# Attention into a soft mixture of experts: other order of the last second-layer weights, a plain output tail, and one weight pair loaded in pieces

## The chip, the core and the metric

The kernel runs on one core of a Trainium2 chip. The core has a matrix engine (PE, TensorE), a vector engine (DVE), a scalar engine (ACT), GpSimd (POOL), a sync engine (SP), and 16 DMA engines that move data between HBM and the on-chip SBUF. Matrix products land in PSUM, which has eight banks here. The metric is the device time of one execution in microseconds (us). Before the change three runs took 179.84, 180.31 and 181.1 us: a median of 180.31.

## The reference

Two stages are computed. The first is attention for 8 batches, 8 heads, 576 positions of 64 elements; four heads see the last 32 positions, four see every fourth of the last 128. The second is a soft mixture of experts over all 4608 tokens (x, 4608x512), with 8 experts of 4 slots each:

```python
logits = x @ phi                                  # 4608 x 32 slots
d = softmax(logits, over tokens); c = softmax(logits, over slots)
slot_input = d.T @ x                              # 32 x 512, 4 slots per expert
for e in range(8):
    h = np.maximum(slot_input[e] @ w1[e], 0.0)    # 512 -> 1024
    slot_out[e] = h @ w2[e]                       # 1024 -> 512
out = c @ slot_out                                # 4608 x 512, float32
```

Nothing of the output can be stored before every token is in `slot_input` and every expert's `w2` has arrived, since each output row mixes all 32 slots. The weights are 16 MB (w1) and 16 MB (w2) in float32 and are cast to bf16 by the transfers that load them; the output is 9.44 MB.

## The kernel before, in words

**Attention part.** Eight units (a pair of batches and a kind of mask each) go through transposes, scores, exponentials, masks, values and logits, with tiles in rotating buffers. The change doesn't touch this part. Its input is loaded unit by unit into three staging buffers (`stg`), all by transfers that POOL issues (`load_unit`, L415).

**Order of the work.** Every operation is entered with the function `op`: engine, what it reads and writes, a guessed cost and a key. A planner (`Prog.schedule`) then simulates the engines and writes out one fixed order for each; of operations that could start within 0.12 us it takes the smallest key. POOL's and SP's operations keep the order in which the program enters them. Where the planner sees PE idle between 116 and 149 us of its own time it puts in filler products (L1052), which compute nothing that is used. Waits are semaphore waits in front of an instruction, on the engine that executes it: whatever stands behind it on that engine waits too.

**Weights.** `wload` (L448) issues one transfer for a whole weight, or one for each listed piece (lo, hi, c0, c1): chunks lo to hi of the 1024 inner rows (8 chunks, each row of 128 partitions holds one per chunk) and columns c0 to c1. Weights go where buffers fall free. `w10` to `w16` have their own place (`WD`); `w17`, `w20` to `w24` use the three staging buffers, two in each; `w25` to `w27` use the attention's transposed tiles (`TT`). The last ones before the change are w25 whole, then for each half of the 512 output columns w26 with all 8 chunks, w27 with chunks 0–5, w27 with chunks 6–7. Behind them POOL issues 15 tiny copies, the "marks" (L782): mark n copies n rows of n elements, and nothing waits for them.

**Second stage.** When the attention is done, the slot inputs are folded (L794) and the first layer is multiplied (L814) into `h_sb`; L852 sums the token weights into `rtok`, and L832 and L841 turn `h_sb` into `hT`. The second layer (`ffn2`, L901) then makes, for each half of the output columns, one PSUM bank `sp_[h]` with the 32 slots: one product for each expert and chunk, 32 rows wide. Experts e and e+4 share one of four column groups of PE. All `ffn2` operations before the change stand in one chain, each after the one before it.

**Output tail before.** The function `half` handles one half of the columns. For chunks 6 and 7 of expert 7 it goes around the second layer: `h7` is scaled from `h_sb` (L871), multiplied with the first 512 tokens (L877) and evicted into `G` (L881, L884). `half` scales the unfinished slot outputs into `so_sb` (L931 or L932), multiplies the first two output groups by it (L957), adds the products of `G` with the late chunks (L960), and stores. Then the late chunks go through `ffn2` as well, rows 96–127 of the slot outputs are scaled once more into `so_fin`, POOL copies the other 96 rows there (L944), and the groups 1 to 5 follow (L989, evicted at L998 or L932). An output group of `half` is 256 tokens; its store (L926, on SP) is half the columns, 256 KB in 1 KB rows. There are six such groups (`NAB`). Last come groups of 512, 512, 1024 and 1024 tokens in full width (L1034), one store each.

Of the kernel before, what the change touches and what calls it, by code (L numbers as in the profile page):

```python
# [7 lines left out]
AluOp = mybir.AluOpType  # L8
# [294 lines left out]
def bass_dilated_sliding_attn__then__soft_moe_slots_kernel(  # L303
# [46 lines left out]
    so_fin = psA_sb[:].bitcast(BF16)[:, 0:DM]  # L350
    m7 = sb("m7", [128, 1], F32)
# [47 lines left out]
    b_m7 = Buf()  # L399
# [345 lines left out]

    W_AFTER = {2: ["w10"], 3: ["w11"], 4: ["w12"], 5: ["w13"], 6: ["w14"],
               7: ["w15", "w16"]}
    for u in range(NU):
        for j in range(4):
            st_T(u, j)  # L750
        if u + 3 < NU:
            for n_ in W_AFTER.get(u + 2, ()):
                wload(n_)
            load_unit(u + 3)
        else:
            if u == 5:
                for n_ in W_AFTER[7]:
                    wload(n_)
            for n_ in {5: ["w17", "w20"], 6: ["w21", "w22"], 7: ["w23", "w24"]}[u]:
                wload(n_)  # L760
        for i in range(6):
            st_S(u, i)
# [11 lines left out]
    for h_ in range(2):  # L774
        sl = (256 * h_, 256 * h_ + 256)
        wload("w26", ((0, 8) + sl,))
        wload("w27", ((0, 6) + sl, (6, 8) + sl))

    mk = sb("mk", [15, 136])
    for n_ in range(1, 16):  # L780
        o_ = sum(range(n_))
        op("pool", lambda g, n_=n_, o_=o_: [g.dma_start(mk[0:n_, o_:o_ + n_], moe_w2[7, 0:n_, 0:n_])],  # L782
           cost=0.3, sem=DmaSem(nc, f"s_mark{n_}"), nbytes=1024)
# [60 lines left out]
    NAB = 6  # L844
    GRP = [2] * NAB + [4, 4, 8, 8]
    rs = tile(psum, 1)

    def rsum(t):
# [13 lines left out]
    op("dve", lambda vv: vv.tensor_reduce(m7[:], ident[:, 100:104], mybir.AxisListType.X, AluOp.add),  # L862
       r=[b_id], w=[b_m7], cost=0.1, key=K1)
    op("dve", lambda vv: vv.tensor_tensor(m7[:], m7[:], rcs[:], AluOp.mult),
       r=[b_rcs], w=[b_m7], cost=0.1, key=K1)
    h7 = tile(pPT)
    G = [tile(pPT), tile(pPT)]

    def so_all(p0=0, p1=128, sl=slice(0, 512)):
        return so_fin[p0:p1, sl]  # L870
    op("dve", lambda vv: vv.tensor_scalar(sbt(h7)[:, 0:256].rearrange("p (f c) -> p f c", c=2),  # L871
                                          h_sb[:].rearrange("p (f c) -> p f c", c=8)[:, :, 6:8],
                                          m7[:, 0:1], None, op0=AluOp.mult),
       r=[b_m7] + b_h, w=[h7], alloc=[h7], cost=0.3, key=K1 + 1.5)
    for c in range(2):
        gp = tile(psum, 1)
        op("pe", lambda t, c=c, gp=gp: t.matmul(bank(gp)[:, 0:NG], sbt(h7)[:, c:256:2], expT[:, 0:NG],  # L877
                                                start=True, stop=True),
           r=[h7] + b_expT[:2], w=[gp], alloc=[gp, G[c]], cost=0.25, key=K1 + 1.6)
        if c == 0:  # L880
            op("act", lambda ac, gp=gp: ac.activation(sbt(G[0])[:, 0:NG], bank(gp)[:, 0:NG], ACTF.Copy),  # L881
               r=[gp], w=[G[0]], cost=0.6, key=K1 + 1.7)
        else:
            op("dve", lambda vv, gp=gp: vv.tensor_copy(sbt(G[1])[:, 0:NG], bank(gp)[:, 0:NG]),  # L884
               r=[gp], w=[G[1]], cost=0.6, key=K1 + 1.7)

# [4 lines left out]
    chain = []  # L891

    def ffn2(es_, lo, hi_, h_, key, after=()):
# [3 lines left out]
        def pe(t):  # L897
            for cc in range(lo, hi_):
# [8 lines left out]
               a=[sp_[h_], b_sp[h_]], cost=0.12 * (hi_ - lo), mode="c", key=key, after=chain[-1:] + list(after))  # L907
        chain.append(o)
# [11 lines left out]
    def store(d0, n, ap, ob, key, h_=None):  # L920
        so = DmaSem(nc, f"s_out{d0}_{h_}")
        s_out.append(so)
        dst = out[d0:d0 + 128 * n, :].rearrange("(p j) f -> p j f", j=n)
        if h_ is not None:
            dst, ap = dst[:, :, CH[h_]], ap[:, :, CH[h_]]
        op("sp", lambda e: [e.dma_start(dst, ap)], r=[ob], cost=0.1, sem=so,  # L926
           nbytes=262144 * n // (1 if h_ is None else 2), key=key)
# [6 lines left out]
    pb7 = {c0: pb for l2, h2, c0, c1, pb in HOME["w27"][1].parts if l2 == 6}  # L934
    AB = [(256 * o, osts[o // 2][:, 1024 * (o % 2):1024 * (o % 2) + 1024].rearrange(
        "p (j f) -> p j f", j=2), b_ost[o // 2]) for o in range(NAB)]
    b_soah = [[Buf(), Buf()] for _ in range(2)]

    def half(h_, key):
        sl = CH[h_]  # L940
        eA, eB = (("dve", "act"), ("act", "dve"))[h_]
        xe = op(eA, lambda en: scaled(en, so_sb[:, sl], bank(sp_[h_])[:, 0:256], rcs[:, 0:1]),
           r=[b_sp[h_], b_rcs, sp_[h_]], w=[b_so[h_]], cost=0.45, key=key)
        op("pool", lambda g: g.tensor_copy(so_all(0, 96, sl), so_sb[0:96, sl]), r=[b_so[h_]],  # L944
           w=[b_soah[h_][0]], after=b_psA.ready + b_psA.reads, cost=0.6, key=key + 0.1)
        po = [tile(psum, 1) for _ in range(3)]
        last = [None, None, None]
        for c in (None, 0, 1):
            for o in range(2):
                for j in range(2):  # L950
                    k_ = j if o == 0 else 2
                    d0 = AB[o][0]

                    def pe(t, o=o, j=j, k_=k_, d0=d0, c=c):
                        d_ = bank(po[k_])[:, CH[j] if o else CH[0]]
                        if c is None:
                            return t.matmul(d_, row(d0, 2)[j], so_sb[:, sl],  # L957
                                            start=o == 0 or j == 0, stop=False,
                                            skip_group_check=True)
                        return t.matmul(d_, sbt(G[c])[:, d0 + j:d0 + 256:2], w2v[7][:, 6 + c, sl],  # L960
                                        start=False, stop=c == 1, skip_group_check=True)
                    x = op("pe", pe, r=[b_so[h_]] + b_expT[:2] if c is None else [G[c], pb7[sl.start]],
                           a=[po[k_]], alloc=[po[k_]] if last[k_] is None else [], cost=0.15,
                           key=key + 1 + (0 if c is None else 1 + o) + 0.1 * j,
                           after=[last[k_]] if last[k_] is not None else [])
                    last[k_] = x
                    if c is not None:
                        HOME["w27"][1].reads.append(x)
        ffn2((7,), 6, 8, h_, key + 3.5, after=[xe])
        d0, ap, prev = AB[0]  # L970
        ob = Buf()
        for j in range(2):
            op(("act", "dve")[j], lambda en, j=j: scaled(
                en, AB[0][1][:, j, sl], bank(po[j])[:, 0:256], rtok[:, j:j + 1]),
               r=[po[j], b_rtok], a=[ob], after=prev, cost=0.4, key=key + 4)
        store(d0, 2, ap, ob, key + 4, h_)
        op(eB, lambda en: scaled(en, so_all(96, 128, sl), bank(sp_[h_])[96:128, 0:256],
                                 rcs[96:128, 0:1]),
           r=[b_sp[h_], b_rcs, sp_[h_]], w=[b_soah[h_][1]], after=b_psA.ready + b_psA.reads, cost=0.4, key=key + 4.1)
        for o in range(1, NAB):  # L980
            d0, ap, prev = AB[o]
            if o == 1:
# [122 lines left out]
```

## Time and profile before

| | |
|---|---|
| runs | 179.84, 180.31, 181.1 us (median 180.31) |
| profiled execution | 180.75 us, its span 179.0 us |
| PE busy | 136.4 us (76%) |
| DVE busy | 116.0 us (65%) |
| ACT busy | 94.1 us (53%) |
| POOL busy | 47.4 us (26%) |
| read from HBM, written | 61.94 MB, 9.44 MB |
| second layer L901 | 145.0 to 156.5 us |
| first store issued, last store issued | 151.55, 167.48 us |
| half-width stores, issue to landing | 3.4 us (median of 12) |

All times of the trace count from the start of the span. "Busy" is the time in which an engine executes; of a DMA transfer the profile gives the time of its issue on the engine that issues it, and the time to its landing. The trace also keeps when each transfer added to its semaphore: 16 additions, one from each DMA engine, so that one can see how far the engines stand apart. In the answers by stretches each row gives the length of the stretch, the busy time of PE, PEld (weight loads of PE), DVE, ACT and POOL, the granted clock of PE, the mean share of the 16 DMA engines, and GB/s.

### The profile page before, as it was taken

How to read it: one execution, taken by the hardware profiler on the slowest of the kernel's cores; microseconds unless marked ns; L12 is line 12 of the kernel's file. 1: busy time of each engine (PE TensorE's matmuls, PEld its weight loads, DVE VectorE, ACT ScalarE, POOL GpSimd, SP SyncE). 2: the span in 40 equal slices, each digit the busy share in tenths (PEclk: the TensorE clock that was granted, in tenths of full speed). 3: DMA queues.
4: the chain of work that ended last, by engine and by line, in shares of the span. 5: the costliest groups of instructions: out<-in, count | busy, mean ns of one | idle time of the engine just before them, and what ended most of it. 6: DMA issues, size and time to landing. Idle time of an engine off the chain costs nothing.

```text
span 179.0 us, 5831 instructions
## 1 busy us (share of the span) xinstructions
PE 136.4 (76%) x2614; PEld 104.3 (58%) x2614; DVE 116.0 (65%) x264; ACT 94.1 (53%) x141; POOL 47.4 (26%) x92
## 2 busy tenths in 40 slices
PE   0019789986988988898998698889999999879000
PEld 0019568865867967676876576865656587533000
DVE  6840297699579589759669669789952233489400
ACT  2004666975765894754895486675330121559300
POOL 7990700600700430620110010023995000000000
PEclk9999999999999999999999999999999999999855
DMA  5999999999999999999999999999999999889996
GB/s 81 192 216 212 216 214 212 222 214 212 219 210 210 217 214 217 208 226 207 220 208 220 211 216 222 212 211 223 212 211 213 194 198 118 251 293 396 421 458 293
DMA packets 13384, 40.81 MB, mean 228 GB/s; under 512 B 2352, under 2 KB 9520, under 8 KB 9520
## 3 DMA queue, kind: packets, MB, share of 16 engines
q0 software_dynamic: 8992, 30.94, 86.9%
q1 hardware_dynamic: 4368, 9.50, 14.1%
q8 instruction: 20, 0.33, 0.7%
q14 instruction: 4, 0.03, 0.0%
HBM read 61.94 MB, written 9.44 MB: 399 GB/s over the span
## 4 chain that ended last, share of the span: by engine, by line
PE 47%; DVE 28%; ACT 9%; DMA 5%; issue 3%; POOL 1%; DVEq 0%; POOLq 0%
DVE XB L651 9%; PE ps L549 7%; DVE PT L601 7%; DMA stg<-in_v_dram 5%; PE ps L544 5%; PE ps L695 5%; PE ps L611 5%; ACT PT L593 4%; PE ps L668 4%; DVE VN L616 4%; PE ps L586 3%; DVE WD L931 3%; PE ps L1052 3%; PE ps L901 3%; ACT TT L568 3%
## 5 line engine op out<-in xcount | busy, mean ns | idle before, releaser
L568 ACT ACTIVATE TT<-ps 128x864 f32<-128x864 f32 x32 | 28.6, 894 | 31.6 <-PE ps L549 22.5
L593 ACT ACTIVATE PT<-ps 128x768 bf16<-128x768 f32 x48 | 37.0, 813 | 8.4 <-PE ps L586 8.1
L549 PE MATMUL ps<-ident,stg 96*64 96x96 bf16 x576 | 18.3, 226 | 16.4 <-DMA stg<-in_v_dram 12.9
L651 DVE TENSOR_TENSOR XB<-ps,RV 96x768 bf16<-96x768 f32 x32 | 30.3, 948 | 0.7
L549 PEld LDWEIGHTS ps<-ident,stg 96*64 96x64 bf16 x576 | 16.0, 124 | 18.0 <-DMA stg<-in_v_dram 12.9
L616 DVE COPY VN<-ps 128x768 bf16<-128x768 bf16 x32 | 17.6, 548 | 11.8 <-PE ps L611 11.8
L415 POOL DMA_DIRECT2D stg<-in_q_dram x16 | 8.4, 533 | 46.1 <-PE ps L549 23.8
L640 PE MATMUL ps<-VN,PT 128*128 128x65 bf16 x384 | 18.1, 195 | 2.3 <-DVE PT L601 0.9
L611 PE MATMUL ps<-ident,TT 128*128 128x128 bf16 x192 | 17.7, 232 | 1.6 <-issue 0.9
L640 PEld LDWEIGHTS ps<-VN,PT 128*128 128x128 bf16 x384 | 14.8, 99 | 4.8 <-DVE PT L601 1.7
L586 PE MATMUL ps<-TT 64*128 64x96 bf16 x384 | 15.8, 211 | 2.0 <-ACT TT L568 1.0
L680 DVE COPY XT<-ps 128x576 bf16<-128x576 bf16 x17 | 10.1, 596 | 10.4 <-PE ps L668 10.3
L611 PEld LDWEIGHTS ps<-ident,TT 128*128 128x128 bf16 x192 | 11.8, 103 | 5.9 <-issue 2.3
L544 PE MATMUL ps<-ident,stg 96*128 96x96 bf16 x288 | 14.9, 206 | 0.2
L668 PE MATMUL ps<-ident,XB 96*128 96x96 bf16 x192 | 12.7, 207 | 2.5 <-DVE XB L651 2.2
L932 ACT ACTIVATE WD<-ps,rtok 128x256 f32<-128x256 f32 (+1 forms) x18 | 8.7, 591 | 9.5 <-PE ps L960 6.7
L586 PEld LDWEIGHTS ps<-TT 64*128 64x128 bf16 x384 | 10.1, 97 | 6.1 <-issue 1.7
L601 DVE TENSOR_TENSOR PT<-PT,mask_d 128x768 bf16<-128x768 bf16 x24 | 13.0, 544 | 0.9 <-ACT PT L593 0.4
L544 PEld LDWEIGHTS ps<-ident,stg 96*128 96x128 bf16 x288 | 13.0, 98 | 0.5 <-ACT PT L593 0.3
L448 POOL DMA_DIRECT2D stg<-in_moe_w_dram x6 | 3.2, 533 | 38.1 <-PE ps L544 25.5
L601 DVE TENSOR_TENSOR PT<-PT,mask_p 128x768 bf16<-128x768 bf16 x24 | 12.7, 541 | 0.4 <-ACT PT L593 0.4
L668 PEld LDWEIGHTS ps<-ident,XB 96*128 96x128 bf16 x192 | 9.5, 98 | 5.1 <-DVE XB L651 4.2
(95 smaller groups left out, 202.3 us busy)
## 6 DMA issues: line engine op xcount, KB each, us to landing
WD<-in_moe_w_dram POOLq DMA_DIRECT2D x7, 1024.0 KB, 26.2
stg<-in_moe_w_dram POOLq DMA_DIRECT2D x6, 1024.0 KB, 21.3
stg<-in_q_dram POOLq DMA_DIRECT2D x16, 288.0 KB, 16.2
stg<-in_k_dram POOLq DMA_DIRECT2D x16, 288.0 KB, 18.1
stg<-in_v_dram POOLq DMA_DIRECT2D x16, 288.0 KB, 20.1
out_dram<-WD SPq DMA_DIRECT2D x12, 256.0 KB, 3.4
out_dram<-WD SPq DMA_DIRECT2D x2, 1024.0 KB, 5.5
out_dram<-WD SPq DMA_DIRECT2D x1, 2048.0 KB, 8.8
```

What stands on the lines that cost most here:

```text
L544: i_ = t.transpose(bankb2(pt, a)[:, 96 * kk:96 * kk + 96], two[:, j // 2, c, :], ident[0:96, 0:96])
L549: i_ = t.transpose(bankb2(pt, a)[64 * hx:64 * hx + 64, 96 * kk:96 * kk + 96], src[:, hx, c, :], ident[0:96, 0:96])
L568: return ac.activation(d, sv, ACTF.Copy)
L586: i_ = t.matmul(pair(sc)[:, hx, QB * x:QB * x + QB], win(u, 1, h01, blk_, bpar)[64 * hx:64 * hx + 64], win(u, 0, h01, blk_, bpar)[64 * hx: ...
L593: op("act", lambda ac: ac.activation(sbt(pt)[:, 0:768].rearrange("p (x n) -> p x n", x=2), pair(sc)[:, :, 0:384], ACTF.Exp, scale=SCALE), ...
L601: return dv.tensor_tensor(p_, p_, m.unsqueeze(1).to_broadcast([128, 2, 384]), AluOp.mult)
L611: i_ = t.transpose(bankb(pv)[:, 128 * m:128 * m + 128], win(u, 2, h01, m, bpar), ident[:, :])
L616: op("dve", lambda dv: dv.tensor_copy(sbt(vn)[:, :, :, 0:64], bankb(pv)[:, 0:768].rearrange("p (m x d) -> p m x d", m=6, x=2)), r=[pv], w= ...
L640: i_ = t.matmul(pair(po)[:, bk, 65 * po_:65 * po_ + 65], sbt(pts[i])[:, o_:o_ + 128], sbt(vn)[:, m, half, 0:65], start=True, stop=True)
L651: op("dve", lambda dv: dv.tensor_tensor(sbt(xb)[:].rearrange("p m (x h d) -> p h x m d", x=2, h=2)[:, h01], pv()[:, :, :, 0:64], sbt(rv)[: ...
L668: i_ = t.transpose(bankb(px)[:, QB * m:QB * m + QB], sbt(xb)[:, m, 128 * x:128 * x + 128], ident[0:QB, 0:QB])
L680: return en.tensor_copy(d, s_)
```

## The change

Four things change.

1. The way around the second layer is taken out: `h7`, `G`, `m7`, `so_fin` and all that makes them. `half` now scales the finished slot outputs once into `so_sb`, and multiplies each group by it. The store of the first group is split in two of 128 KB.
2. `half` has five groups instead of six. A group of 256 tokens in full width (512 KB, 4 KB rows) stands ahead of the full-width groups.
3. The `ffn2` operations stand in a chain for each half, in smaller steps, and the last ones of the second half (expert 6's chunks 6–7, expert 7) are made dependent on the products of the first half's groups (`after=mm0`). w26 and w27 are loaded in other pieces.
4. The pair w23, w24 is loaded by `wpair` in six transfers in place of two: chunks 0–5 of both whole, then chunks 7 and 6 by rows, in pieces of 26, 102, 34 and twice 94 rows. Between them stand three tiny copies of 2, 2 and 7 rows (`turn`).

```diff
+    def turn(n):
+        i = len(turns)
+        turns.append(n)
+        op("pool", lambda g: [g.dma_start(
+            mk[0:n, i, :, 0:2],
+            moe_w2[7, 0:n, :].rearrange("p (a x) -> p a x", a=4)[:, 0:2, 0:2])],
+           w=[Buf()], cost=0.3, sem=DmaSem(nc, f"s_turn{i}"), nbytes=256)
+
+    def wpair(na, nb, s_, steps):
...
+        v_ = moe_w2[e0:e0 + 2].rearrange("e (p c) f -> p e c f", c=8)
+        d_ = stg[:, s_, 0:8192].rearrange("p (e c f) -> p e c f", e=2, c=8)
+        for n, st in enumerate(steps):
+            if isinstance(st, int):
+                turn(st)
+                continue
+            r0, r1, c0, c1, x = st
...
+            o = op("pool", lambda g, src=src, dst=dst: [g.dma_start(dst, src)],
+                   after=pb.prev, a=[pb], cost=0.6, sem=DmaSem(nc, f"s_{na}_{n}"),
...
-            for n_ in {5: ["w17", "w20"], 6: ["w21", "w22"], 7: ["w23", "w24"]}[u]:
+            for n_ in {5: ["w17", "w20"], 6: ["w21", "w22"], 7: []}[u]:
                 wload(n_)
+            if u == 7:
+                wpair("w23", "w24", 1, (
+                    (0, 128, 0, 6, None), (102, 128, 7, 8, None), 2, (0, 102, 7, 8, None), 2,
+                    (0, 34, 6, 7, None), 7, (34, 128, 6, 7, 0), (34, 128, 6, 7, 1)))
...
     wload("w25")
-    for h_ in range(2):
-        sl = (256 * h_, 256 * h_ + 256)
-        wload("w26", ((0, 8) + sl,))
-        wload("w27", ((0, 6) + sl, (6, 8) + sl))
+    wload("w26", ((0, 6, 0, 512), (6, 8, 0, 256)))
+    wload("w27", ((0, 4, 0, 256), (4, 8, 0, 256)))
+    wload("w26", ((6, 8, 256, 512),))
+    wload("w27", ((0, 4, 256, 512), (4, 8, 256, 512)))
...
-    NAB = 6
-    GRP = [2] * NAB + [4, 4, 8, 8]
+    NAB = 5
+    GRP = [2] * NAB + [2, 4, 4, 8, 8]
...
     def half(h_, key):
         sl = CH[h_]
+        mm = []
+        e0, e1 = (("dve", "act"), ("act", "dve"))[h_]
+        op(e0, lambda en: scaled(en, so_sb[:, sl], bank(sp_[h_])[:, 0:256], rcs[:, 0:1]),
            r=[b_sp[h_], b_rcs, sp_[h_]], w=[b_so[h_]], cost=0.45, key=key)
...
+        for o in range(NAB):
...
+            if o == 0:
                 for j in range(2):
...
+                    mm.append(op("pe", lambda t, j=j, p1=p1: t.matmul(
+                        bank(p1)[:, 0:256], row(0, 2)[j], so_sb[:, sl], start=True, stop=True),
+                        r=[b_so[h_]] + b_expT, w=[p1], alloc=[p1], cost=0.15, key=k2))
...
+                    store(d0, 2, ap, ob, k2, h_, j)
+                continue
...
+            mm.append(op("pe", pe, r=[b_so[h_]] + b_expT, w=[p2], alloc=[p2], cost=0.25, key=k2))
...
+            store(d0, 2, ap, ob, k2, h_)
+        return mm
+
+    for h_ in range(2):
+        k_ = K1 + 2 + 0.5 * h_
+        ffn2((0, 1, 2, 3), 0, 8, h_, k_)
+        ffn2((4, 5), 0, 4, h_, k_ + 2)
+        ffn2((4, 5), 4, 8, h_, k_ + 2.1)
+        ffn2((6,), 0, 6, h_, k_ + 4)
+    ffn2((6,), 6, 8, 0, K1 + 10)
+    ffn2((7,), 0, 4, 0, K1 + 11)
+    ffn2((7,), 4, 8, 0, K1 + 12)
+    mm0 = half(0, K1 + 20)
+    ffn2((6,), 6, 8, 1, K1 + 30, after=mm0)
+    ffn2((7,), 0, 4, 1, K1 + 31)
+    ffn2((7,), 4, 8, 1, K1 + 32)
     half(1, K1 + 40)
```

In the order that the planner writes for the changed kernel, all engines do the same as before up to the second layer. From there PE has five filler products ahead of the second layer instead of two products of `h7` and two fillers, and none ahead of the first output products, where three stood. Ahead of the first half's scaling now stand 118 second-layer products instead of 110. SP has 17 stores instead of 16.

## The prediction

> **What bounds the kernel now.** I read the slices of the whole span first, then the timeline of the tail, then the transfers' share by stretches. The slices:
>
> ```profile
> DMA  5999999999999999999999999999999999889996
> GB/s 81 192 216 212 216 214 212 222 214 212 219 210 210 217 214 217 208 226 207 220 208 220 211 216 222 212 211 223 212 211 213 194 198 118 251 293 396 421 458 293
> ```
>
> The 16 DMA engines are full from start to end but for the slices around 150 us (a slice is 4.5 us). Up to there they load (input bytes are counted after the cast to bf16); behind it they store 9.44 MB. The end is therefore the start of the stores, plus their transfer time, plus every hole in the stream. The timeline of the tail shows start and hole:
>
> ```profile
> 148.41 0.96 PE L901 MATMUL ps<-TT,hT 128*32 128x256 bf16 x12
> ...
> 149.41 0.48 DVE L931 TENSOR_SCALAR so_sb<-ps,rcs 128x256 bf16<-128x256 f32 x1 [4.03 <-PE ps L901]
> ...
> 150.40 1.04 PE L960 MATMUL ps<-TT,PT 128*128 128x256 bf16 x8
> 150.82 0.47 ACT L932 ACTIVATE WD<-ps,rtok 128x256 f32<-128x256 f32 x1 [5.75 <-PE ps L960]
> ...
> 151.55 13.63 SPq L926 DMA_DIRECT2D out_dram<-WD  x15
> ...
> 156.51 0.69 DVE L998 TENSOR_TENSOR WD<-ps,rtok 128x512 f32<-128x512 f32 x1
> 157.23 0.49 DVE L931 TENSOR_SCALAR psA_sb<-ps,rcs 32x256 bf16<-32x256 f32 x1
> 157.78 1.05 PE L989 MATMUL ps<-psA_sb,expT 128*128 128x256 bf16 x8 [0.99 <-DVE psA_sb L931]
> 158.21 1.29 DVE L998 TENSOR_TENSOR WD<-ps,rtok 128x512 f32<-128x512 f32 x2 [0.49 <-PE ps L989]
> ```
>
> The reader is to see two detours. In half 0 the slot outputs (so_sb) are ready to be scaled at 149.41, but the first store is issued only at 151.55, since the side products L960 lie between. In half 1 the outputs are scaled twice: DVE makes rows 96–127 again at 157.23, PE multiplies at 157.78, DVE evicts at 158.21. The stretches show what this does to the transfers (the last two figures are DMA share and GB/s):
>
> ```profile
> 157.00:159.00 2.00, 1.22 (x10) 0.93 (x10) 1.48 (x4) 0.57 (x2) 0.00 (x0) 1.00 1.04 349
> 159.00:161.00 2.00, 1.94 (x10) 0.81 (x8) 2.00 (x4) 2.00 (x5) 0.00 (x0) 1.00 0.66 223
> 161.00:163.00 2.00, 2.00 (x9) 0.67 (x8) 2.00 (x4) 2.00 (x5) 0.00 (x0) 1.00 1.04 345
> 163.00:168.00 5.00, 2.48 (x9) 0.78 (x8) 4.41 (x7) 3.94 (x7) 0.00 (x0) 1.00 1.05 429
> ```
>
> Half-width stores run at some 345 GB/s, full-width ones at 429, and between 159 and 161 a third of the time is lost. The trace's landing records (each transfer adds to its semaphore once per DMA engine) agree. The stores' landings are 153.9, 154.7, 155.8, 156.5, 157.3, 158.1, 158.9, 159.6, then 161.2, 162.0, 162.7, 163.5: 0.76 us apart, with holes of 0.35 (third) and 0.85 (ninth). The 1 MB stores follow at 2.5 us each, the 2 MB ones at 4.9 each; the last lands at 178.54.
>
> **The loads.** The same records show sixteen engines that do not finish together. Whole weights take 4.86 us per engine. w25 lands on eight engines from 138.27 to 139.45, on the other eight from 140.56 to 142.34; the last piece of w27 from 148.93 to 150.12 and from 151.50 to 153.06.
>
> **The change, part by part.**
>
> *Pieces of w23 and w24.* Chunks 6 and 7 of the pair are 512 reads of 2 KB, 32 per engine before. Now 8x34=272 go to eight engines and the other 240 to all, 15 each: 49 against 15. A read costs 76 ns (4.86 us/64 in a whole load) to 83 (two of the 512-byte packets, of which 64 took 2.67 us); I take 80. So 17x80 ns=1.36 us more on eight engines, and less on eight. Which eight, no row of before tells. If they are the early ones, w25 lands at 139.6–140.8 and 139.2–141.0; I take this, but an even spread leaves the sum as it is, as the cover below shows. Eight more small transfers stand in the queue. The nearest rows are the closing marks: their packets follow each other on an engine by 0.03 us, their landings by 0.18. That makes 0.2 to 1.4 us; I take 0.2, since the first store's data landed only 0.16 us behind the last mark on the late engines, so data does not wait in that line. w25 is in at 141.2 instead of 142.3. On POOL nine issues replace two: about 9x0.55=5 us from 117.44, done by 122.5, before w25's at 123.83 (which waits for PE); the engines hold earlier loads until 123.7. It costs nothing.
>
> *Order of w26 and w27.* Half 0 now needs 0.75 weight at whole-load speed (3.65 us) and 0.625 in 512-byte packets (5.34 us a weight, so 3.34) behind w25: 141.2+7.0=148.2 against 147.7 before. The last load lands 3.34 later, at 151.5 instead of 153.06.
>
> *Half 0 on PE.* Gone are G (two products of 0.22), h7, two evictions and POOL's copies; three more filler products of 0.22 stand in their place, so the second products start 0.2 later than 145.01. Ahead of the scaling now lie expert 6's chunks 0–5 of half 1 as well (6 matmuls) and 7's chunks 6–7 (2). Matmuls of one expert follow by 0.109 us; experts use separate column groups, and group 7 began some 0.4 us before 6 ended. Expert 6: 14 from 148.30, last at 149.72; expert 7: 8 from 149.4, last at 150.18; scaling 0.31 later, at 150.5 instead of 149.4. Bounds: 150.0 if 7 overlaps fully, 151.2 if not at all. The pieces that this waits for landed 1.6 us before their use; that is the cover. Without it each us of lateness is one of the end.
>
> *First stores.* 150.5+0.48 (scaling)+0.07+0.33 (product to eviction)+0.47=151.85; the first store issues at 151.9, 0.35 later than now, but with 128 KB. The next is another 128 KB; SP's price for that form is unknown, between 0.33 (128 rows) and 0.62 (256 rows), I take 0.45. The third (256 KB) issues at 152.85 and lands 2.25 later (1.5+0.755) at 155.1, and from there the transfers set the pace: SP issues every 0.62, ACT and DVE deliver two stores in about 0.8.
>
> *Half 1.* Ten half-0 products stand in front on PE's queue (the added dependency): 151.05 to 152.15; behind them wait ten FFN products, done by 153.3; ACT ends its evictions at 153.45 and scales until 154.05; product and eviction until 155.0; SP is free at 155.4. The stream would run dry only for an issue after 155.9. So the hole goes, and SP, then the transfers, are late next.
>
> *The sum.* Third store 155.1; three more, 157.4; half 1, 2x0.38+4x0.755, 161.15; the new 512 KB group 1.25 (a quarter of 4.9 to two half-width, 1.51), 162.4; 2x2.5, 167.4; 2x4.9, 177.2. That is 1.3 us before 178.54. The profiled execution took 180.75 (span 179.0 and 1.75 around it), so 179.45; it lies 0.44 above the median of 180.31, hence 179.0 there.
>
> **A rule against the rows.** The closing marks number the engines: mark n is n rows of 2n bytes, and the records hold n such packets, one per engine. By these, engines 0–4, 7 and 8 reached them at 148.6–149.9, 5, 6 and 9–14 at 151.3–152.9; 15, without data, is then the eighth early one. The Trainium skill ("DMA: Bandwidth & Descriptors", latency and other measured facts) says instead that engines 7 and 15 are usually the slow ones. By its section on why a DMA adds 16, a transfer takes the largest divisor of its rows up to 16 as its number of engines, from a rotating cursor: 26, 2, 102, 2, 34 rows from engine 0 put the 34-read shares on 15, 0–4, 7 and 8. By the rows these are the early eight, and the sum stands; by the rule on 7 and 15 two would be late, with half 0 in at about 150.9 and some 180.1 us. I go by the rows.
>
> **The rivals.**
>
> 1. *The change doesn't do what it says: no rebalancing, or the wrong eight.* Even spread: half 0 in at 142.34+0.2+7.0=149.5, still ahead of its use at 149.8. Late eight: 142.34+1.36+0.2+7.0=150.9, scaling at 151.65, 1.15 later: 180.1. 14%.
> 2. *More gain.* Experts 6 and 7 overlap fully, scaling at 150.0, and SP's short issues cost 0.33: 1.9 us, 178.4. If the half-width stores also go at 0.67 us apart, as the late engines did while they caught up (landings from 156.4 to 160.4), the eight 256 KB' worth of them behind the third store save 0.7 more: 177.7. For it: separate column groups. Against it: the 0.4 us of overlap seen, and the 0.76 of the other engines. 20%.
> 3. *Slower: reads piled on a late engine.* If the 94-row pieces go to two engines each, those take 47 reads more, 3.8 us. On a late engine half 0 lands at 142.34+3.8+0.2+7.0=153.3, scaling at 154.1, 3.6 later: +2.3, 182.6. It decides from a landing after 149.8, and makes the kernel slower from 151.1 on. 8%.
>
> **How the numbers follow.** Forecast 179.0, its own range 178.4 to 179.8, 58%. Range for 8 in 10: 177.7 to 181.0, from the second rival's best to the first's worst. One per cent (1.8 us) is about what a measurement here tells from no change: the three runs span 179.84 to 181.1. Faster by over 1% (under 178.5): rival 2 and the forecast's edge, 0.25. Slower by over 1% (over 182.1): rival 3, 0.07. The rest 0.68.
>
> **What would show it.** Landings of w25 within 2 us; scaling of half 0 at 150.5; first store at 151.9; no dip of the DMA share between 155 and 163; twelve landings without a hole; last landing at 177.2. Wrong it would be if half 0 waits for a landing, if 128 KB stores cost SP the full 0.62, or if the stores' pace changes.

## The result, and the profile after

The changed kernel took 178.68 us (median of seven runs, 178.51 to 179.21), the kernel before 179.87 us (seven runs, 179.46 to 181.1; the three known beforehand are among them). The ratio is 0.9912, with a 95% interval of 0.9883 to 0.994: 0.9% less time. Runs more than 1.5% above the fastest of their kernel are left out of the medians, ranges and ratios of this document. The profiled execution of the changed kernel took 178.78 us with a span of 177.0, against 180.75 and 179.0 before. In the profile after, the second layer is L912, the scaling L944 or L945, the products of `half` L962 and L975, its evictions L944, L945 and L987, the stores L939.

The slices of the whole span, transfers only (an average slice is 4.4 us now):

```profile
DMA  5999999999999999999999999999999999899996
GB/s 71 200 212 216 210 219 212 214 215 212 219 216 211 217 210 211 223 208 216 217 212 216 217 215 213 220 213 216 212 210 200 212 194 194 196 357 416 446 437 296
```

The valley of the profile before, 118 GB/s around 150 us and 251 and 293 behind it, is gone: the lowest value there is 194, and the next step is 357 at once. The stretches of the tail (length; busy time of PE, PEld, DVE, ACT and POOL; clock; share of the 16 DMA engines; GB/s):

```profile
151.00:153.00 2.00, 1.54 (x14) 0.71 (x11) 1.27 (x3) 1.59 (x5) 0.00 (x0) 1.00 0.69 120
...
157.00:159.00 2.00, 1.91 (x8) 0.64 (x8) 2.00 (x4) 2.00 (x5) 0.00 (x0) 1.00 1.06 356
159.00:161.00 2.00, 1.91 (x7) 0.65 (x8) 2.00 (x4) 2.00 (x5) 0.00 (x0) 1.00 1.06 392
```

The stretch from 159 to 161, where the transfers' share was 0.66 before, now has 1.06. One weak stretch is left, from 151 to 153. The timeline shows what stands at its front:

```profile
145.40 1.70 PE L912 MATMUL ps<-TT,hT 128*32 128x256 bf16 x14 [0.34 <-DMA TT<-in_moe_w_dram]
147.41 0.61 PE L912 MATMUL ps<-TT,hT 128*32 128x256 bf16 x4 [0.31 <-DMA TT<-in_moe_w_dram]
148.93 0.61 PE L912 MATMUL ps<-TT,hT 128*32 128x256 bf16 x4 [0.90 <-DMA TT<-in_moe_w_dram]
149.57 0.48 DVE L944 TENSOR_SCALAR so_sb<-ps,rcs 128x256 bf16<-128x256 f32 x1 [8.73 <-PE ps L912]
150.11 0.39 PE L962 MATMUL ps<-so_sb,expT 128*128 128x256 bf16 x2 [0.58 <-DVE so_sb L944]
...
150.94 9.74 SPq L939 DMA_DIRECT2D out_dram<-WD  x15
...
152.13 0.61 PE L912 MATMUL ps<-TT,hT 128*32 128x256 bf16 x4 [0.21 <-DMA TT<-in_moe_w_dram]
152.78 0.47 ACT L945 ACTIVATE so_sb<-ps,rcs 128x256 bf16<-128x256 f32 x1 [0.41 <-PE ps L912]
```

Before, each half had two scalings: half 0 at 149.41 and (rows 96–127) at 151.79, half 1 at 154.44 and 157.23. Now there is one in each half, the products follow it 0.54 us later, and the first store issues 1.37 us behind the scaling, where 2.14 us lay between. But three groups of the second layer now stand behind a weight that is still in flight (the brackets: 0.34, 0.31 and 0.90 us idle, ended by a DMA from `in_moe_w_dram`). The chain of waits, asked for the stretch from 120 to 160 us (start, duration, what), says the same:

```profile
120.00 4.72 POOL TT L445 x7
124.72 27.37 DMA TT<-in_moe_w_dram
152.09 0.04 issue
152.13 0.62 PE ps L912 x4
```

It runs along the loads alone, from their issue on POOL to the last landing at 152.09, and only then enters PE. In the profile before loads and PE changed places: DMA had 5% of the whole chain and PE 47%; here DMA has 21% and PE 27%.

### The profile page after: what moved, and what is told of

The parts are those of the page before. It is cut to its first block, busy times and chain, and to the rows that moved or that the text cites. A ratio compares the mean times of both kernels' runs of the same rounds, so it can differ in the third digit from the quotient of the medians.

```text
span 177.0 us, 5782 instructions
## 1 busy us (share of the span) xinstructions
PE 132.5 (75%) x2589; PEld 101.0 (57%) x2594; DVE 113.1 (64%) x258; ACT 93.0 (53%) x140; POOL 51.8 (29%) x98
## 4 chain that ended last, share of the span: by engine, by line
DVE 29%; PE 27%; DMA 21%; ACT 9%; POOL 4%; issue 2%; DVEq 0%; POOLq 0%
DMA TT<-in_moe_w_dram 15%; DVE XB L648 9%; DVE PT L598 8%; PE ps L546 5%; DMA stg<-in_v_dram 5%; PE ps L541 5%; ACT PT L590 4%; DVE VN L613 4%; PE ps L692 4%; ACT TT L565 4%; DVE WD L944 3%; PE ps L608 3%; POOL TT L445 3%; PE ps L665 3%; PE ps L583 3%
## 5 line engine op out<-in xcount | busy, mean ns | idle before, releaser
L637 PE MATMUL ps<-VN,PT 128*128 128x65 bf16 x384 | 17.6, 194 | 2.7 <-DVE PT L598 1.2
L608 PE MATMUL ps<-ident,TT 128*128 128x128 bf16 x192 | 16.3, 221 | 0.7 <-DVE VN L613 0.5
L583 PE MATMUL ps<-TT 64*128 64x96 bf16 x384 | 15.3, 204 | 1.2 <-ACT TT L565 1.0
L945 ACT ACTIVATE WD<-ps,rtok 128x256 f32<-128x256 f32 (+1 forms) x19 | 9.1, 605 | 10.3 <-PE ps L962 10.3
L608 PEld LDWEIGHTS ps<-ident,TT 128*128 128x128 bf16 x192 | 10.8, 98 | 4.7 <-issue 1.6
L583 PEld LDWEIGHTS ps<-TT 64*128 64x128 bf16 x384 | 9.6, 94 | 5.2 <-ACT TT L565 1.2
L678 ACT ACTIVATE XT<-ps 128x576 bf16<-128x576 bf16 x15 | 9.8, 650 | 3.8 <-PE ps L665 3.5
```

Of the source, the lines that this page charges most:

```text
L583: i_ = t.matmul(pair(sc)[:, hx, QB * x:QB * x + QB], win(u, 1, h01, blk_, bpar)[64 * hx:64 * hx + 64], win(u, 0, h01, blk_, bpar)[64 * hx: ...
L608: i_ = t.transpose(bankb(pv)[:, 128 * m:128 * m + 128], win(u, 2, h01, m, bpar), ident[:, :])
L637: i_ = t.matmul(pair(po)[:, bk, 65 * po_:65 * po_ + 65], sbt(pts[i])[:, o_:o_ + 128], sbt(vn)[:, m, half, 0:65], start=True, stop=True)
```

## The experiments

Two readings were set against each other. By the prediction's own, PE sets when half 0 is finished, the loads have 1.6 us of cover, and the pieces of w23 and w24 are worth nothing. By the other, which the profile after suggests, the last load of half 0 sets it, and the pieces are worth what they bring it forward. All ratios are against the kernel before on the same chip; its median was between 179.77 and 179.97 us in each group.

### The pieces taken out (e1_plainpair)

```diff
-                wpair("w23", "w24", 1, (
-                    (0, 128, 0, 6, None), (102, 128, 7, 8, None), 2, (0, 102, 7, 8, None), 2,
-                    (0, 34, 6, 7, None), 7, (34, 128, 6, 7, 0), (34, 128, 6, 7, 1)))
+                wload("w23")
+                wload("w24")
```

> The changed kernel with one part undone: w23 and w24 are loaded whole again (two transfers, no pieces, no turns). Theory A, the one of the prediction (the gain is the tail's: one scaling, no side products, no hole; the loads are covered): the time stays at the changed kernel's, 178.7 us, and half 0 is scaled at the same time as in it. Theory B (in the changed kernel PE waits 0.9 us for w27's last piece of half 0, so the loads set the start of the stores): the late eight engines end some 1.2 us later, half 0 is scaled at 150.8 instead of 149.57, and the time is 179.8 us.

Measured: 179.5 us (nine runs, 179.21 to 179.55), ratio 0.9967 (0.9953 to 0.998). The timeline of this kernel:

```profile
149.65 0.61 PE L911 MATMUL ps<-TT,hT 128*32 128x256 bf16 x4 [0.69 <-DMA TT<-in_moe_w_dram]
150.30 0.48 DVE L943 TENSOR_SCALAR so_sb<-ps,rcs 128x256 bf16<-128x256 f32 x1 [8.40 <-PE ps L911]
```

w25 again lands over 4.1 us (138.52 to 142.57) instead of 1.2 (140.25 to 141.43), the last load of half 0 at 149.61 instead of 148.88, and everything behind it moves by that 0.73: scaling 150.30, last landing 177.31 instead of 176.58. That is less than the 1.2 us of theory B, but its mechanism: the loads set half 0, and the pieces are worth 0.7 us here (0.8 by the medians), not nothing.

### The same pieces for the other eight engines (e2_wrong8)

```diff
-                    (0, 128, 0, 6, None), (102, 128, 7, 8, None), 2, (0, 102, 7, 8, None), 2,
-                    (0, 34, 6, 7, None), 7, (34, 128, 6, 7, 0), (34, 128, 6, 7, 1)))
+                    (0, 128, 0, 6, None), 6, (102, 128, 7, 8, None), 2, (0, 102, 7, 8, None), 2,
+                    (0, 34, 6, 7, None), 9, 8, (34, 128, 6, 7, 0), (34, 128, 6, 7, 1)))
```

Only the tiny copies between the pieces differ; their row counts set which engines the next piece goes to.

> The changed kernel with other turns (6 ahead of the 26 rows, 9 and 8 instead of 7 behind the 34 rows), so that the 34-read shares should fall on engines 5-10, 13 and 14: six of the eight that were late before, and two early ones. Theory A: 178.7 to 179.5 us. Theory B: w25's slowest landing goes from 141.4 to about 144, half 0 is scaled 2.5 us later, and the time is about 181.2 us. If the shares don't follow the turns, the landings of w25 look like those of the changed kernel.

Measured: 181.29 us (five runs, 181.15 to 181.42), ratio 1.0072 (1.0058 to 1.0087). The timeline:

```profile
151.45 0.61 PE L912 MATMUL ps<-TT,hT 128*32 128x256 bf16 x4 [0.78 <-DMA TT<-in_moe_w_dram]
152.10 0.48 DVE L944 TENSOR_SCALAR so_sb<-ps,rcs 128x256 bf16<-128x256 f32 x1 [7.63 <-PE ps L912]
```

w25 lands from 137.50 to 143.20, the last load of half 0 at 151.40, and the end moves by the same 2.5 us, as theory B had it. With the reads on six of the eight late engines and two early ones the kernel is slower than before: the prediction's first rival exists, at 181.3 instead of the 180.1 reckoned.

### The new tail over the old order of loads (e3_tailonly, e4_oldorder)

Both put the loads of w26 and w27 back to one half after the other; e3 also takes the pieces out as in e1. PE's order stays that of the changed kernel.

```diff
-    wload("w26", ((0, 6, 0, 512), (6, 8, 0, 256)))
-    wload("w27", ((0, 4, 0, 256), (4, 8, 0, 256)))
-    wload("w26", ((6, 8, 256, 512),))
-    wload("w27", ((0, 4, 256, 512), (4, 8, 256, 512)))
+    for h_ in range(2):
+        sl = (256 * h_, 256 * h_ + 256)
+        wload("w26", ((0, 8) + sl,))
+        wload("w27", ((0, 4) + sl, (4, 8) + sl))
```

> The new tail alone: w23 and w24 whole, w26 and w27 in the order of before (half 0 complete first, then half 1). Theory A: 178.7 us or less. Theory B: half 0 is complete at 147.7, so the first store is issued at about 149.9, but half 1's last load comes at 153.1 and its first store at 155.2, after the stream has run dry for 1.2 us: 178.9 us.

> The changed kernel with the pieces of w23 and w24, but w26 and w27 in the order of before (half 0 complete first). Theory A: no change, 178.7 us. Theory B: half 0 complete at 147.0 (141.4 and 5.3 for one weight in 512-byte packets), first store at about 149, last load at 152.1, half 1's first store at 154.3 instead of 154.5; a hole of about 1 us in the stream, but its end 0.7 us earlier: 178.0 us.

Measured: e3 181.14 us (five runs, 181.02 to 182.49; ratio 1.0091, 1.006 to 1.0122), e4 180.82 us (six runs, 180.22 to 181.22; ratio 1.005, 1.0033 to 1.0068). Both are far from what either reading gave. The timeline of e4 shows why for that kernel:

```profile
149.46 1.50 PE L912 MATMUL ps<-TT,hT 128*32 128x256 bf16 x16 [0.78 <-DMA TT<-in_moe_w_dram]
151.00 0.48 DVE L944 TENSOR_SCALAR so_sb<-ps,rcs 128x256 bf16<-128x256 f32 x1 [6.78 <-PE ps L912]
```

PE still has expert 6's chunks 0–5 of *half 1* ahead of half 0's last products. In the old order of loads that weight lands late (149.42), so half 0 waits for a load of half 1. These two edits did not undo one part; they broke a pair: the order of the loads and the order of the products must be changed together (the next two runs do that, and are 1.7 and 1.9 us faster). For e3 the profiled execution (184.0 us) had PE late for another reason, told at the end, so its wait is not shown there.

### The pair kept together (e5_tail2, e6_order2)

Both use the old order of loads with a fitting order of products; e5 without the pieces, e6 with them.

```diff
-        ffn2((6,), 0, 6, h_, k_ + 4)
-    ffn2((6,), 6, 8, 0, K1 + 10)
+    ffn2((6,), 0, 8, 0, K1 + 10)
...
-    ffn2((6,), 6, 8, 1, K1 + 30, after=mm0)
+    ffn2((6,), 0, 8, 1, K1 + 30, after=mm0)
```

> The new tail alone, now with PE's order made to fit the loads of before: w23 and w24 whole, w26 and w27 half by half, and all of expert 6's second half behind the first half's products (in the earlier run its chunks 0-5 stood ahead of them and waited for a load of half 1). Theory A (the gain is the tail's): half 1's last load at 153.1 sets its first store to 155.2, 0.7 us later than in the changed kernel, which delays the end by 0.25: 178.9 us. Theory C (the gain is the loads' alone: their order and their balance): 179.9 us, as before.

> The changed kernel (with the pieces) with w26 and w27 half by half and PE's order to fit. Theory B (loads set the start of the stores): half 0 complete at 147.0, scaled at 147.8 to 149.4 as PE arrives, last load 152.1, half 1's first store at 154.3 against 155.1 in the profile of the changed kernel; 178.0 us. Rival: the order of the loads only moves a wait from half 0 to half 1, 178.7 us.

Measured: e5 179.46 us (twelve runs, 179.29 to 181.01; ratio 0.9989, 0.9964 to 1.0013), between the ends written down, and not told apart from the kernel before; e6 178.9 us (seven runs, 178.68 to 179.2; ratio 0.9939, 0.9918 to 0.9961). So the new tail without the pieces is worth 0.3 us by the medians (179.46 against 179.77; the interval allows 0.65), and the pieces add 0.6. For e6 theory B's 178.0 did not come, its rival's 178.7 nearly did. In e6 the first store issues at 148.72, 2.2 us before that of the changed kernel, yet nothing is gained, and its last load lands later (152.37 against 152.09). The timeline of e6:

```profile
150.21 1.44 PE L912 MATMUL ps<-TT,hT 128*32 128x256 bf16 x12 [1.04 <-DMA TT<-in_moe_w_dram]
152.41 0.61 PE L912 MATMUL ps<-TT,hT 128*32 128x256 bf16 x4 [0.77 <-DMA TT<-in_moe_w_dram]
153.06 0.47 ACT L945 ACTIVATE so_sb<-ps,rcs 128x256 bf16<-128x256 f32 x1 [2.92 <-PE ps L912]
```

Half 1 waits for its loads, and is scaled 0.28 us later than in the changed kernel; its first store issues as early (154.43 against 154.46). The trace shows where the early start is lost. The first packets of the first store start 1.9 us after its issue (150.63), against 0.85 in the changed kernel (151.79) and 0.84 in e1: the store starts only as the loads leave the first of the DMA engines (last load landed there at 150.72). And the engines end apart: the last store is done on the first of the sixteen at 175.98, 0.40 earlier than in the changed kernel (176.38), but on the last one at 176.80, 0.82 later than on the first (0.20 in the changed kernel). So an engine that is still behind sets the end; I take it to be one that was late with the loads. The 15 marks stand on every engine between loads and stores; no run takes them out of e6, so their part in this is open.

### Six half-width groups as before (e7_nab6)

```diff
-    NAB = 5
-    GRP = [2] * NAB + [2, 4, 4, 8, 8]
+    NAB = 6
+    GRP = [2] * NAB + [4, 4, 8, 8]
```

On top of e6.

> As the one with order and pieces, and with six half-width groups instead of five, so that half 0 has 0.76 us more of stores to cover the wait for half 1's last load, at a price of 0.13 for each half (256 KB in 1 KB rows 0.76, in full width 0.63). Theory B: the hole of 0.9 us is filled, 177.6 us. Rival (no hole to fill): 0.26 us slower than the run with five.

Measured: 178.86 us (twelve runs, 178.74 to 180.56), ratio 0.9947 (0.9923 to 0.997): the same as e6. Theory B's 177.6 did not come, and the rival's 0.26 us is not seen either: the sixth group per half against the 512 KB group makes no difference that can be seen.

### The pieces in the old kernel (e8_before_pieces)

The kernel before, with `turn` and `wpair` and the call of `wpair` put in, and nothing else.

> The kernel before with the pieces of w23 and w24 alone. Theory A (loads are covered there): half 0 is scaled at 149.41 while its loads are in at 147.72, and half 1 waits for ACT and for its second scaling, so nothing changes: 179.9 us. Theory B (the slowest engine's landing counts in it as well): as much as the pieces gave in the changed kernel, 0.8 us: 179.1 us.

Measured: 179.92 us (ten runs, 178.88 to 180.82), ratio 0.999 (0.9956 to 1.0024). The pieces alone give nothing that can be measured, though the interval still allows theory B's 0.8 us. The profile speaks for theory A: half 0 is scaled 4.39 us after the second layer starts (143.66 to 148.05), as before (145.01 to 149.41), with its loads in at 146.59. The stretches show the old hole, its end 1.36 us earlier than in the profile before (landing 159.84 against 161.20):

```profile
155.00:157.00 2.00, 1.01 (x10) 0.63 (x9) 1.48 (x4) 0.00 (x0) 0.00 (x0) 1.00 1.07 371
157.00:159.00 2.00, 1.94 (x12) 1.00 (x10) 2.00 (x4) 1.92 (x5) 0.00 (x0) 1.00 0.74 259
159.00:161.00 2.00, 2.00 (x9) 0.63 (x6) 2.00 (x4) 2.00 (x5) 0.00 (x0) 1.00 1.05 347
```

### The binding taken out (e9_nodep)

```diff
-    ffn2((6,), 6, 8, 1, K1 + 30, after=mm0)
+    ffn2((6,), 6, 8, 1, K1 + 30)
```

> The changed kernel without the added dependency: the second half's last FFN products no longer wait for the first half's output products, and the planner puts them ahead of these on PE. If the binding matters as the traces suggest (half 1's last load comes at 152.1, after which PE needs 0.6 us): half 0's first output product at about 152.8 instead of 150.1, its first store at 153.6 instead of 150.9, and the time 2.0 to 2.6 us more, 180.7 to 181.3 us. Rival (the DMA engines are full of loads until 152.1 anyway, so an earlier store only displaces a load): 178.7 to 179.3 us.

Measured: 181.62 us (four runs, 181.11 to 181.88), ratio 1.0092 (1.007 to 1.0113): 2.8 us above the changed kernel on the same chip (178.80), a little more than expected. The timeline:

```profile
149.52 0.48 DVE L944 TENSOR_SCALAR so_sb<-ps,rcs 128x256 bf16<-128x256 f32 x1 [5.82 <-PE ps L912]
150.84 0.61 PE L912 MATMUL ps<-TT,hT 128*32 128x256 bf16 x4 [0.97 <-DMA TT<-in_moe_w_dram]
152.12 0.61 PE L912 MATMUL ps<-TT,hT 128*32 128x256 bf16 x4 [0.68 <-DMA TT<-in_moe_w_dram]
152.67 0.39 PE L962 MATMUL ps<-so_sb,expT 128*128 128x256 bf16 x2
...
153.64 2.81 SPq L939 DMA_DIRECT2D out_dram<-WD  x5
```

and its stretches:

```profile
151.00:153.00 2.00, 1.32 (x11) 0.77 (x10) 0.00 (x0) 0.23 (x1) 0.00 (x0) 1.00 0.17 13
153.00:155.00 2.00, 2.00 (x19) 1.57 (x16) 1.90 (x4) 2.00 (x7) 0.00 (x0) 1.00 0.21 69
```

Half 0 is scaled at 149.52, as early as in the changed kernel (149.57). But PE's queue now has the last products of half 1 first, these wait for their own loads until 152.12, and the first output product comes at 152.67, 2.6 us later. Nothing is stored before 153.64 (13 GB/s from 151 to 153). Of the edits of a single part this one costs most (2.7 us at the last landing, against 2.5 in e2): the binding keeps ready work from standing behind work that waits.

### The marks taken out (e10_nomarks), and both kernels again (e11_after_again, e12_before_again)

e10 is the changed kernel without the 15 tiny copies behind the loads; they compute nothing. e11 and e12 are the two kernels unchanged.

```diff
-    for n_ in range(1, 16):
-        o_ = sum(range(n_))
-        op("pool", lambda g, n_=n_, o_=o_: [g.dma_start(mkt[0:n_, o_:o_ + n_], moe_w2[7, 0:n_, 0:n_])],
-           cost=0.3, sem=DmaSem(nc, f"s_mark{n_}"), nbytes=1024)
```

> The changed kernel without the 15 closing marks (tiny copies that nothing reads). They stand on every engine between its last load and its first store: 0.4 us at the spacing of their packets (0.028 us), 2.6 us at the spacing of their landings (0.17 us). If only the packets' time counts: 178.4 us. If the stores wait for the marks' landings: 177 us or less. If the first store's issue (150.9) sets the pace and the engines stand idle then anyway: 178.7 us.

> The changed kernel once more, for a second profile and on the chip of the two others: 178.7 us. Theory: PE comes to the second layer between 141 and 145 us, as its clock was slow for some us or not at all in the attention part, and the end doesn't depend on it, since PE then waits for the loads. Rival: an execution with a slow spell ends later by the 1.5 to 3 us that the spell costs.

> The kernel before once more, for a second profile. The first one's PE ran slowly from 20.4 to 25.6 us, and its second layer began at 145.0. If such spells differ from execution to execution, this one may begin at 141 to 145; then half 0 is scaled at 147.9 at the earliest (its loads are in at 147.7), and the end is 178.5 or at most 1 us earlier, since half 1's detour and last load (153.1) stay.

Measured: e10 178.99 us (ten runs, 178.41 to 180.82; ratio 0.9962, 0.9928 to 0.9996), e11 178.80 us (eleven runs, 178.47 to 180.65, nine of them below 179; ratio 0.9944, 0.9912 to 0.9976), e12 180.74 us (one run). e12's second layer began at 145.0 once more, with its slow spell elsewhere; e11's profile had no spell, so it can't tell its theory from its rival. Five of e10's runs lie near 178.5, three near 180.6 and two at 179.3, so no effect of the marks is shown; its fastest run rules out the branch of 177 us or less. Its profiled execution (180.59 us) is the one with PE late, and the loads are long in when PE gets there:

```profile
146.12 2.03 PE L906 MATMUL ps<-stg,hT 128*32 128x256 bf16 x65
...
151.39 0.48 DVE L938 TENSOR_SCALAR so_sb<-ps,rcs 128x256 bf16<-128x256 f32 x1 [5.83 <-PE ps L906]
```

From the first product of the second layer to the scaling are 5.27 us without a wait for a load. Here PE set the start of the stores, as the prediction had it, and the end came 1.8 us later than in the first profile after.

### All profiled executions in one table

The first three columns are read from the timelines and the landing records, the last is the difference of the two before it.

| kernel | second layer starts | half 0 scaled | first store issues | last landing | first store to end |
|---|---|---|---|---|---|
| before | 145.0 | 149.41 | 151.55 | 178.54 | 26.99 |
| before again (e12) | 145.0 | 149.42 | 151.56 | 178.54 | 26.98 |
| before with pieces (e8) | 143.7 | 148.05 | 150.19 | 177.19 | 27.00 |
| after | 141.4 | 149.57 | 150.94 | 176.58 | 25.64 |
| after again (e11) | 141.9 | 149.20 | 150.56 | 176.34 | 25.78 |
| without pieces (e1) | 142.4 | 150.30 | 151.66 | 177.31 | 25.65 |
| other eight (e2) | 145.0 | 152.10 | 153.46 | 179.10 | 25.64 |
| old load order (e4) | 144.8 | 151.00 | 152.36 | 178.02 | 25.66 |
| old load order, no pieces (e3) | 149.5 | 154.79 | 156.15 | 181.78 | 25.63 |
| without binding (e9) | 144.2 | 149.52 | 153.64 | 179.29 | 25.65 |
| without marks (e10) | 146.1 | 151.39 | 152.75 | 178.40 | 25.65 |
| fitted order, no pieces (e5) | 144.2 | 148.78 | 150.14 | 177.22 | 27.08 |
| fitted order, pieces (e6) | 142.5 | 147.35 | 148.72 | 176.80 | 28.08 |
| fitted order, six groups (e7) | 144.5 | 149.09 | 150.45 | 176.99 | 26.54 |

The table carries most of the case. The old tail takes 27.0 us from its first store, wherever that is. The new tail takes 25.65 us in seven executions whose first stores issue anywhere from 150.9 to 156.2: the tail's own gain is 1.34 us. What is left is when the first store can issue, and that is set by whichever is later, PE or the loads of half 0 (in e9 by what stands ahead on PE's queue). From some 150.6 down an earlier first store is given back (e5 to e7). In these three the last store ends 0.78 to 0.85 us later on the last DMA engine than on the first, against 0.20 in the changed kernel; in e5 and e6 half 1 also waits 0.79 and 0.77 us for its last load. The measured time is 2.2 us above the last landing in every row that I compared (178.78 − 176.58, 180.75 − 178.54, 181.29 − 179.10).

## Why the prediction was right, and where its steps were not

The forecast was 179.0 us with a range of 177.7 to 181.0; the time was 178.68 us. The mechanism was right for the tail. What sets the start of the stores was wrong: half 0 waits for a landing, which the prediction itself names as a sign of being wrong. PE came earlier than reckoned and the loads later; that the later of the two still came within 0.9 us of the forecast is luck.

- **The hole: right.** Share 1.06 where 0.66 stood, and twelve half-width landings without a gap. From the third store to the last of half 1 (154.17 to 160.24, on the engine that lands first) are 6.07 us, where the sum had 6.05 (155.1 to 161.15). The 512 KB group took 1.3 us (1.25 reckoned), the rest 14.8 (14.8).
- **Scaling to first store: right.** 1.37 us (1.4 reckoned). The 128 KB stores cost SP 0.35 and 0.43 us (0.45) in half 0; in half 1 they cost 0.61 and 0.48, and no gap follows. From the first store to the end the sum had 25.3 us. It follows the stores on the engine that lands first, where the runs show 25.44; the table's 25.65 is the last engine's. So its 177.2 was to be compared with 178.35, where the first engine ended before, and not with 178.54: the gain that it reckoned is 1.15 us, not 1.3.
- **PE's products of half 0: right where they could be seen.** 5.3 us from 145.2 to 150.5 were reckoned; e10 shows 5.27, as the assumed overlap of experts 6 and 7 gives. Full overlap, part of the second rival, did not come.
- **Start of the second layer: wrong.** 145.2 was taken from the one profiled execution; the changed kernel's profile has 141.4. The change itself moved it the other way by the 0.2 us reckoned: from the last product of the first layer to the first of the second are 3.35 us before and 3.56 after. The step took as fixed what changes between executions (see the last section). This alone would have made half 0 ready at 146.7.
- **The loads' cover: wrong.** The step "the pieces that this waits for landed 1.6 us before their use; that is the cover" fails. The load was 0.7 us later than reckoned (148.88 against 148.2; 0.2 of it in w25, at 141.43 against 141.2, the rest behind it, 7.45 us against 7.0, though 7.01 on the engine that lands first), and PE came 3.8 us earlier. PE waits 0.90 us instead. Half 0 is scaled at 149.57, 0.9 us earlier than forecast; the end comes 0.8 earlier (176.38 on the first engine, against 177.2).
- **The small transfers.** Nine issues in place of two are seven more, not eight. That the first store's data landed 0.16 us behind the last mark does not show that data passes the marks: in e6, where the first store is issued 2.2 us earlier, it lands 0.18 to 0.20 us behind the last mark all the same. Whether the marks cost time stays open.
- **"An even spread leaves the sum as it is": wrong, for the same reason.** e1 puts the pieces at 0.7 us. "It costs nothing" stands for POOL: nine issues from 113.6 to 119.7 (6.1 us), w25's at 120.0, without delay.
- **Which eight engines: right.** The landing records show the additional reads, 34 of them in 2.67 us on an engine (78.5 ns each), on exactly the eight early ones, and w25 within 1.2 us. e2 shows the price of the other choice, 181.3 us, where the first rival had 180.1: the load of half 0 came in at 151.40, not 150.9; the tail behind it took 0.3 us more than the sum; and the 0.44 us by which the profile before lay above its median were taken off, which this kernel's profile does not have (181.29, as its median).
- **The 94-row pieces: the third rival falls.** They cost every engine 0.2 to 0.45 us; none took 47 reads.
- **The binding.** The prediction named what is queued behind it, and gave it no value of its own. e9 shows 2.8 us: it is the condition under which the other gains hold.
- **Profile against median.** The forecast of −1.3 us was worked out between profiled executions, where −1.97 was measured (180.75 to 178.78): 0.61 by an earlier first store, where 0.35 later was forecast, and 1.35 behind it. The medians differ by 1.19. Between profiles the forecast was 179.45 and thus 0.67 too high; the 0.44 us taken off for the median brought it to within 0.32, but the changed kernel's profile lies only 0.10 above its median. That closeness is luck too. By medians I estimate the first store at 150.7 before and 150.8 after (the time less 2.2 us and less 26.99 or 25.64): nearly all of the 1.19 is the tail's own gain.

The rule of the Trainium skill that the prediction weighed ("DMA: Bandwidth & Descriptors", on why a DMA adds 16) gave the right engines: the divisor of the rows and the rotating cursor put the larger shares where the records then show them. The same page's sentence that engines 7 and 15 are usually the slow ones does not hold here: engine 7 reached its mark at 148.8 in the trace before, among the earliest, where the late ones came at 151.3 to 152.9 (engine 15 has no mark).

What the parts are worth, by medians: the old tail 179.8 to 180.0 us, with the pieces 179.92; the new tail with a fitting order of loads and products 179.46 to 179.5, with the pieces 178.7 to 178.9. Alone, the tail gives 0.3 to 0.5 us and the pieces nothing that shows; together they give 0.9 to 1.2.

## What to carry to other kernels

When a stream of stores ends a kernel, measure the time from the first store to the end apart from the time to the first store: the first is the tail's own and repeats to some 0.02 us as long as the loads have left the DMA engines, the second belongs to whichever of engines and loads is late, and a gain in one can hide a change in the other. Cover that is read from one profiled execution is only as firm as the start that it is counted from; compute both arrivals, and ask what happens if the engine is a few us earlier. Where an engine's queue holds both ready work and work that waits for a load, put the ready work first and tie the rest behind it, and change the order of loads together with the order of their use.

## What the runs showed of the hardware that I had not expected

The attention part is the same code in all these kernels, and yet the second layer behind it started anywhere from 141.4 to 149.5 us. The traces show spells of 3 to 5 us in which PE's matmuls follow each other more slowly than usual. The same instructions, first in the profile before, then after:

```profile
19.85 0.50 PE L586 MATMUL ps<-TT 64*128 64x96 bf16 x8 [1.00 <-ACT TT L568]
20.29 0.82 PE L611 MATMUL ps<-ident,TT 128*128 128x128 bf16 x6
```

```profile
20.00 0.35 PE L583 MATMUL ps<-TT 64*128 64x96 bf16 x8 [0.99 <-ACT TT L565]
20.29 0.51 PE L608 MATMUL ps<-ident,TT 128*128 128x128 bf16 x6
```

0.50 us against 0.35, 0.82 against 0.51; the two groups come back every 1.19 us instead of every 0.72. The spell lasted from 20.4 to 25.6 us in the profile before and from 44.8 to 48.2 in e12. e2 and e10 had one from 20 to 25, e4, e5 and e9 one around 100 to 104, e3 three of them, e7 one at 76 to 79; the profiles of after, e1, e6, e8 and e11 had none. I estimate 1.5 to 2.6 us of lost matmul time for each, from the longer distances between equal matmuls. It does not explain every difference: e8 had no spell and started its second layer at 143.7, 2 us later than the changed kernel did.

The granted clock tells what the spells are. In e12, the column behind the busy times:

```profile
41.40:44.80 3.40, 1.80 (x48) 1.42 (x45) 1.42 (x3) 1.06 (x3) 0.15 (x1) 1.00 1.01 210
44.80:48.20 3.40, 3.40 (x36) 2.46 (x36) 1.56 (x5) 2.12 (x5) 3.38 (x7) 0.50 1.05 220
```

All six traces with a spell behind 40 us have such records, of 0.50 for 3.41 to 3.42 us each, just where the matmuls are slow: e12 from 44.80, e3 from 46.84 and 104.87, e4 from 100.49, e5 from 99.53, e7 from 75.79, e9 from 99.89. In e12's spell the groups of above take 0.50 and 0.82 us again, and the 128x128 products follow each other by 107 ns, where they do by 56 ns at 1.00. For the spells at 20 to 25 us there is no record: the trace's first one, of 1.00, begins at 25.67 in the profile before (25.9 to 26.4 in e2, e10 and e3), at 16.8 to 18.9 in the ten others, and the 1.00 printed ahead of it is no measurement. The distances there are the same 107 and 56 ns. So PE runs at half its clock in these spells.

The Trainium skill ("TensorE: Matmul & The Clock Gate", on the clock gate) describes a gate that lets PE run at half or full rate by how busy it was in a free-running window, and the records of 0.50 agree with the half rate. It says that the number of slow matmuls at a start varies from run to run, as the first records do here (16.8 to 26.4 us), and it warns that the gate's trace events are unreliable; here the distances bear them out. What makes the clock fall no run tested. Ahead of the drops in e12 and e4 PE was busy for 1.80 of 3.40 and 1.76 of 3.39 us; in the profile after, where e4 drops, for 2.85 of 3.39. But e11 has 1.78 of 3.40 (146.9 to 150.3) and no drop, so that alone does not decide it.

In the changed kernel such a spell costs little as long as the loads are later, and shows once PE is later than they are (e10: second layer at 146.1, 1.8 us at the end). That may be why the runs of e11 are either close to 178.7 or above 180.5; the profiles of the runs in between would be needed to show it.
